# A new order for the first 259 of 1788 steps of a GLA recurrence followed by a hard-swish feed-forward

## Chip, cores and metric

The kernel runs on one core of one Trainium2 chip. The metric is device time in microseconds for one execution; the time before is the median of three runs.

## What is computed

A gated linear attention recurrence over 32 (batch, head) pairs, then a feed-forward layer with a hard-swish between two matrix products. All arrays are float32.

```python
for t in range(S):                         # B,H,S,D = 4,8,768,48
    state = alpha[:, :, t, :, None] * state + k_t (outer) v_t
    y[:, :, t] = q_t @ state
x = y.transpose(0, 2, 1, 3).reshape(3072, 384)
h = x @ w_in                               # 384 x 2048
g = h * np.clip(h + 3.0, 0.0, 6.0) / 6.0
out = g @ w_out                            # 2048 x 384
```

The kernel receives its inputs as 64-bit floats; their bit patterns are loaded and the weights are turned into float32 on the chip. That is what the `d` steps below do.

## The kernel before

The sequence is cut into 24 chunks of 128 tokens (`j`, six to a batch entry), and pairs of chunks are the 12 groups `g` of the feed-forward part. There are no loops at run time: the whole kernel is a list of 1788 words, and each word such as `tk.3.1` names a step (a small function) with its arguments. Python walks the list once and emits each step's instructions; each engine then runs its own instructions in the order of the list, and semaphores join the engines. So the list is at the same time the order on TensorE (PE), VectorE (DVE), ScalarE (ACT), GpSimd (POOL) and in SyncE's DMA queue (SP). The list stands in `run("""...""")` at L755; the table of steps is at L732.

The steps of the opening, with the line their instructions carry in the profile:

| word | engine | line | what it does |
|---|---|---|---|
| `la.j lk.j lq.j` | SP | L251, from j=6 L262 | load alpha, k, q of a chunk (192 KB) into a ring of three places; from j=6 four DMAs each |
| `lv.j.z` | SP | L272 | load v in two halves of 96 KB |
| `w.i` | SP | L162, L166 | load slice i of 16 weight slices (768 KB) into one of five landing places |
| `z.m.n` | PE | L532 | n idle matmuls of the identity, two instructions each |
| `ta tk tq .j.bank` | PE | L282 | transpose alpha, k, q into a PSUM bank |
| `ca.j` | ACT | L300 | copy transposed alpha to SBUF (from j=6 on DVE, L286) |
| `r.j`, `p.j` | DVE | L309, L320 | scans of decay and growth, both inputs in SBUF |
| `k.j`, `q.j` | DVE | L332 | scale k and q, read from PSUM in the opening |
| `kb.j`, `ck.j` | PE, ACT | L374, L378 | transpose scaled k back, copy it out |
| `sc.j`, `m.j` | PE, DVE | L346, L356 | scores, masked from PSUM |
| `qa.j.b`, `sv.j.b` | ACT | L366, L419 | place q and the state (`sv.0.0`: POOL, L415) |
| `u.j`, `sm.j.b`, `st.j` | PE, DVE, POOL | L429, L437/L439, L409 | state update |
| `ya yb`, `cy.j` | PE, ACT | L455, L464 | attention output, copied to xT |
| `d1 d2 dx .i` | ACT | L186, L196, L191 | low bits, magnitude, sign of a weight slice |
| `d3.i` | DVE | L203+L205 for slices 0, 1, 2, 4; L207+L208+L210 for the others | high bits |
| `d4.i` | POOL | L217 | integer add that ends the conversion and frees the landing place |
| `fa fb .i`, `f.g.i` | PE | L489, L478 | first product of the feed-forward, by half or whole group |
| `fr.g.i`, `fg.g.i` | ACT, DVE | L494, L498 | clip and gate |

Slices 0 to 7 are `w_in`, 8 to 15 `w_out`. Landing places are shared: `w.5` follows `w.0`, `w.8` follows `w.5`, `w.11` follows `w.8`, `w.14` follows `w.11` in place 0; `w.6`, `w.9`, `w.12`, `w.15` in place 1 and `w.7`, `w.10`, `w.13` in place 2 likewise, so such a load waits in SP's queue, with everything behind it, for the `d4` of the slice before. Four PSUM banks serve the attention steps and four the feed-forward (last number of the word). `qa.0.0` emits nothing.

The lines that walk the list:

```python
    def run(words):
        for word in words.split():
            name, *at = word.split(".")
            steps[name](*(int(x) for x in at))
```

Of the kernel before, what the change touches and what calls it, by code (L numbers as in the profile page):

```python
# [17 lines left out]
def kernel(  # L18
# [42 lines left out]
    G = 2  # L61
# [692 lines left out]
    with tc.manual_schedule():  # L754
        run("""z.0.5 z.0.3 z.0.1 z.0.8 qa.0.0 w.0 d2.0 d3.0 la.0 ta.0.0 ca.0 r.0 lk.0 tk.0.1 k.0  # L755
               z.0.2 p.0 la.1 ta.1.2 lq.0 tq.0.3 ca.1 r.1 lk.1 lv.0.0 sv.0.0 d1.0 kb.0.0 ck.0 z.0.2
               u.0.2.1 sm.0.0 sv.0.1 q.0 qa.0.1 tk.1.0 k.1 p.1 z.0.2 sc.0.2.3 m.0 la.2 ta.2.0 ca.2
               dx.0 w.2 d2.2 kb.1.0 ck.1 lq.1 r.2 sm.0.1 st.1 tq.1.2 q.1 d3.2 z.0.3 d1.2 dx.2
               lv.1.1 u.1.3.1 sv.1.0 sm.1.0 p.2 sm.1.1 sc.1.0.2 m.1 ya.0.3 yb.0 cy.0 lq.2 w.1 d1.1
               tq.2.1 q.2 d4.2 lk.2 tk.2.3 k.2 fa.2.0 d4.0 st.2 sc.2.0.2 d2.1 d3.1 m.2 dx.1 d4.1  # L760
               qa.1.1 lk.3 la.3 ta.3.1 ca.3 la.4 fa.0.1 sv.1.1 w.3 r.3 ta.4.3 ca.4 r.4 tk.3.1 k.3
               kb.2.0 qa.1.0 d2.3 ya.1.2 yb.1 cy.1 fa.1.2 lq.3 ck.2 d1.3 p.3 d3.3 lv.2.2 u.2.3.2
               sm.2.0 d4.3 fb.2 tq.3.1 q.3 fb.1 qa.2.0 sm.2.1 sv.2.0 st.3 fr.0.2.0 fg.0.2 lk.4
               tk.4.0 sv.2.1 w.5 d2.5 k.4 d3.5 d1.5 qa.3.0 d4.5 qa.2.1 sc.3.1.3 m.3 w.6 d2.6 d1.6
               d3.6 d4.6 lv.3.0 lq.4 w.7 kb.3.2 fb.0 f.0.3.3 kb.4.0 ya.2.1 ck.3 u.3.3.2 sm.3.0
# [173 lines left out]
```

## Time and profile before

| | us |
|---|---|
| median of three runs (537.22 to 537.84) | 537.36 |
| profiled execution, whole time | 537.71 |
| its span, first to last instruction | 535.6 |
| PE busy | 523.6 |
| DVE busy | 475.1 |
| ACT busy | 259.7 |
| POOL busy | 50.4 |
| granted TensorE clock, mean | 1.000 |

Busy times are sums over an engine's instructions; matmuls are pipelined and their ends are modelled, so a busy PE need not be at its peak. The opening that the change reorders ends on PE with `fa.4.3` (a group of L489 at 73.34 to 74.84 us) and on VectorE with `fg.1.6` (L498, 72.65 to 73.3 us). In the first 95 us the DMA engines move 20.0 MB, mostly 768 KB weight slices and 192 KB loads of the first chunks. Timeline rows give the start, the time taken, the engine, the line, the operation and its operands; in square brackets stands the idle time before and what ended it.

### The profile page before, as it was taken

The page shows a single profiled execution, that of the slowest core. Times are in us where ns is not written, and L with a number is a line of the kernel's source. Part 1 is how long each engine was busy: PE and PEld are TensorE (multiplying, and loading weights), DVE is VectorE, ACT ScalarE, POOL GpSimd, SP SyncE. Part 2 cuts the span into 40 slices and gives each one's busy share as a digit, 9 for nine tenths or more (in the row PEclk, how much of TensorE's full clock was granted, in tenths as well). Part 3 has the DMA queues.
Part 4 walks back from the last instruction along what each step waited for, and adds up shares of the span by engine and source line. Part 5 has one row for each costly group of instructions (what it writes and reads, how often), then busy time and mean ns, then how long its engine had stood idle before and what let it go on. Part 6 is the DMA issues. An engine that isn't in the chain of part 4 may idle for free.

```text
span 535.6 us, 15166 instructions
## 1 busy us (share of the span) xinstructions
PE 523.6 (98%) x6306; PEld 497.0 (93%) x6306; DVE 475.1 (89%) x839; ACT 259.7 (48%) x513; POOL 50.4 (9%) x71
## 2 busy tenths in 40 slices
PE   7799999999999999999999999999999999999997
PEld 7698886789999999999999999999999999999996
DVE  6999989999999899989999899999999898595381
ACT  3889864302753644543644444642634545553240
POOL 5333435000000000000010000000000000000000
PEclk9999999999999999999999999999999999999999
DMA  9998877006515155254354355055354042100001
GB/s 175 214 250 263 205 218 164 9 1 162 151 28 121 29 120 134 51 139 90 92 118 104 89 122 141 20 126 124 85 137 103 17 97 48 43 3 1 15 16 37
DMA packets 124100, 54.40 MB, mean 102 GB/s; under 512 B 83328, under 2 KB 116864, under 8 KB 124032
## 3 DMA queue, kind: packets, MB, share of 16 engines
q1 hardware_dynamic: 124032, 53.44, 42.4%
q8 instruction: 49, 0.80, 0.7%
q14 instruction: 19, 0.16, 0.1%
HBM read 44.50 MB, written 8.91 MB: 100 GB/s over the span
## 4 chain that ended last, share of the span: by engine, by line
PE 64%; DVE 20%; SPq 5%; DMA 3%; issue 3%; ACT 2%; POOL 2%; DVEq 0%; ACTq 0%; POOLq 0%
PE m_ps L703 28%; PE m_ps L600 24%; PE m_ps L478 4%; SPq L262 3%; PE t_ps L455 3%; DVE R L309 2%; DVE g_sb L498 2%; DVE A L356 2%; DMA v<-in_v_dram 1%; PE t_ps L346 1%; PE m_ps L516 1%; PE t_ps L429 1%; DVE g_sb L537 1%; DVE q L332 1%; DVE t L286 1%
## 5 line engine op out<-in xcount | busy, mean ns | idle before, releaser
L703 PE MATMUL m_ps<-w,g_sb 128*128 128x192 f32 x704 | 122.1, 327 | 0.7 <-ACT m_ps L709 0.6
L606 ACT COPY g_sb<-m_ps 128x512 f32<-128x512 f32 x110 | 63.5, 584 | 113.8 <-PE m_ps L600 97.4
L703 PEld LDWEIGHTS m_ps<-w,g_sb 128*128 128x128 f32 x704 | 113.7, 190 | 1.8 <-ACT m_ps L709 0.9
L703 PE MATMUL m_ps<-rings,g_sb 128*128 128x192 f32 x528 | 91.6, 327 | 0.6 <-ACT u L682 0.6
L703 PEld LDWEIGHTS m_ps<-rings,g_sb 128*128 128x128 f32 x528 | 85.3, 190 | 1.0 <-ACT u L682 0.9
L600 PE MATMUL m_ps<-xc,w 128*128 128x128 f32 x640 | 82.8, 277 | 0.5 <-DVE w L541 0.5
L600 PEld LDWEIGHTS m_ps<-xc,w 128*128 128x128 f32 x640 | 77.5, 192 | 1.7 <-issue 0.6
L494 ACT ACTIVATE r<-g_sb,half 128x512 f32<-128x512 f32 x80 | 56.7, 722 | 29.5 <-DVE g_sb L541 11.7
L498 DVE SCALAR_TENSOR_TENSOR g_sb<-r,g_sb 128x512 f32<-128x512 f32 x80 | 53.6, 683 | 7.2 <-ACT r L494 6.8
L600 PE MATMUL m_ps<-xT,raw 128*128 128x128 f32 x400 | 52.6, 278 | 1.0 <-ACT g_sb L606 0.9
L600 PEld LDWEIGHTS m_ps<-xT,raw 128*128 128x128 f32 x400 | 48.6, 192 | 2.0 <-ACT g_sb L606 1.4
L409 POOL TENSOR_TENSOR st<-sm,R 128x192 f32<-128x192 f32 x20 | 12.9, 644 | 354.4 <-DVE sm L439 305.6
L647 DVE TENSOR_TENSOR g_sb<-g_sb 128x512 f32<-128x512 f32 (+1 forms) x55 | 42.0, 792 | 1.4 <-PE m_ps L703 1.1
L600 PE MATMUL m_ps<-xT,w 128*128 128x128 f32 x320 | 42.0, 276 | 0.0
L600 PEld LDWEIGHTS m_ps<-xT,w 128*128 128x128 f32 x320 | 39.3, 192 | 0.1
L366 ACT COPY A<-q 48x256 f32<-48x256 f32 x88 | 35.6, 404 | 4.9 <-DVE q L332 3.7
L356 DVE TENSOR_TENSOR A<-t_ps,mask 64x256 f32<-64x256 f32 x96 | 36.0, 413 | 0.4
L478 PE MATMUL m_ps<-xT,w 128*128 128x256 f32 x144 | 32.8, 382 | 0.1
L600 PE MATMUL m_ps<-xc,raw 128*128 128x128 f32 x240 | 31.8, 276 | 0.0
L309 DVE TENSOR_TENSOR_SCAN R<-t,ones 128x516 f32<-128x516 f32 x24 | 29.6, 1235 | 1.1 <-ACT t L300 1.0
L478 PEld LDWEIGHTS m_ps<-xT,w 128*128 128x128 f32 x144 | 26.7, 190 | 3.8 <-POOL w L217 0.2
L600 PEld LDWEIGHTS m_ps<-xc,raw 128*128 128x128 f32 x240 | 29.6, 192 | 0.1
(105 smaller groups left out, 724.8 us busy)
## 6 DMA issues: line engine op xcount, KB each, us to landing
raw<-in_moe_w_out_dram SPq DMA_DIRECT2D x8, 768.0 KB, 5.2
raw<-in_moe_w_in_dram SPq DMA_DIRECT2D x6, 768.0 KB, 6.7
v<-in_v_dram SPq DMA_DIRECT2D x48, 96.0 KB, 3.0
out_dram<-oh SPq DMA_DIRECT2D x44, 96.0 KB, 1.7
far<-kq SPq DMA_DIRECT2D x64, 64.0 KB, 2.2
kb<-far SPq DMA_DIRECT2D x64, 64.0 KB, 2.0
aq<-in_alpha_dram SPq DMA_DIRECT2D x36, 96.0 KB, 2.4
qq<-in_q_dram SPq DMA_DIRECT2D x36, 96.0 KB, 2.4
```

The source lines that it names most:

```text
L262: nc.sync.dma_start(out=to[BLK * o : BLK * (o + 1), :, 0 : V * D - skip], in_=t[o // 2, :, :, skip : V * D])
L309: nc.vector.tensor_tensor_scan(out=reverse(R, n - 1, n), data0=reverse(ax, n, n), data1=reverse(ones, n, n), initial=0.0, op0=ALU.mult, op ...
L356: nc.vector.tensor_tensor(out=to[:, a], in0=sc[a][half], in1=mask[half, half].unsqueeze(1).to_broadcast([HB, NP, HB]), op=ALU.mult)
L366: nc.scalar.copy(out=to[:, a], in_=Q_t[j][64 * a : 64 * a + D, :, half])
L455: nc.tensor.matmul(y_of(j, (i + 1) // 2, p)[:, HB * b : HB * b + HB], vb[:, p, e : e + 32], A_t[j][:, b, 2 * p + a], start=(b == 0 and i = ...
L478: nc.tensor.matmul(h[:, f], w1[:, kk, o : o + C], xT_t[g][:, kk], start=(kk == 0), stop=(kk == KT - 1))
L494: nc.scalar.activation(out=to, in_=h, func=AF.Relu, bias=half, scale=1.0 / 6.0)
L498: nc.vector.scalar_tensor_tensor(out=to, in0=r, scalar=1.0, in1=h, op0=ALU.min, op1=ALU.mult)
L600: nc.tensor.matmul(acc[g][i][:, f * C : (f + 1) * C], spots[w][:, f * C : (f + 1) * C], x_of(g, x), start=(first and f == 0), stop=last, s ...
L606: nc.scalar.copy(out=slots[z], in_=acc[g][i])
L647: nc.vector.tensor_tensor(out=out, in0=in0, in1=in1, op=ALU.subtract)
L703: nc.tensor.matmul(to[g], a, rhs[:, f], start=(first and f == 0), stop=(last and f == HF - 1), skip_group_check=True)
```

## The change

The first 259 words of the list are put into another order. The words are the same, with the same arguments (so the same PSUM banks and buffers); from `sv.4.1` on the list is the same, and only its line breaks differ. Each engine thus gets the same instructions, in another order. Before, the reordered words were:

```diff
-        run("""z.0.5 z.0.3 z.0.1 z.0.8 qa.0.0 w.0 d2.0 d3.0 la.0 ta.0.0 ca.0 r.0 lk.0 tk.0.1 k.0
-               z.0.2 p.0 la.1 ta.1.2 lq.0 tq.0.3 ca.1 r.1 lk.1 lv.0.0 sv.0.0 d1.0 kb.0.0 ck.0 z.0.2
-               u.0.2.1 sm.0.0 sv.0.1 q.0 qa.0.1 tk.1.0 k.1 p.1 z.0.2 sc.0.2.3 m.0 la.2 ta.2.0 ca.2
-               dx.0 w.2 d2.2 kb.1.0 ck.1 lq.1 r.2 sm.0.1 st.1 tq.1.2 q.1 d3.2 z.0.3 d1.2 dx.2
-               lv.1.1 u.1.3.1 sv.1.0 sm.1.0 p.2 sm.1.1 sc.1.0.2 m.1 ya.0.3 yb.0 cy.0 lq.2 w.1 d1.1
-               tq.2.1 q.2 d4.2 lk.2 tk.2.3 k.2 fa.2.0 d4.0 st.2 sc.2.0.2 d2.1 d3.1 m.2 dx.1 d4.1
-               qa.1.1 lk.3 la.3 ta.3.1 ca.3 la.4 fa.0.1 sv.1.1 w.3 r.3 ta.4.3 ca.4 r.4 tk.3.1 k.3
-               kb.2.0 qa.1.0 d2.3 ya.1.2 yb.1 cy.1 fa.1.2 lq.3 ck.2 d1.3 p.3 d3.3 lv.2.2 u.2.3.2
-               sm.2.0 d4.3 fb.2 tq.3.1 q.3 fb.1 qa.2.0 sm.2.1 sv.2.0 st.3 fr.0.2.0 fg.0.2 lk.4
-               tk.4.0 sv.2.1 w.5 d2.5 k.4 d3.5 d1.5 qa.3.0 d4.5 qa.2.1 sc.3.1.3 m.3 w.6 d2.6 d1.6
-               d3.6 d4.6 lv.3.0 lq.4 w.7 kb.3.2 fb.0 f.0.3.3 kb.4.0 ya.2.1 ck.3 u.3.3.2 sm.3.0
-               fr.0.3.1 fg.0.3 fr.0.1.0 fg.0.1 qa.3.1 sv.3.0 sm.3.1 p.4 d2.7 sv.3.1 d1.7 d3.7 d4.7
-               f.0.5.0 fr.0.5.1 fr.0.0.0 fg.0.5 fg.0.0 tq.4.3 ck.4 la.5 ta.5.2 f.0.6.3 ca.5 w.4
-               d2.4 ya.3.0 yb.3 cy.3 fr.0.6.1 yb.2 cy.2 w.9 d2.9 q.4 qa.4.1 d1.4 d1.9 dx.4 la.6 w.8
-               d3.4 r.5 lk.5 w.10 d3.9 p.5 ca.6 fg.0.6 d4.9 w.12 lq.5 lv.4.1 d2.8 d3.8 f.0.7.2 d1.8
-               st.4 d4.8 d4.4 w.11 fr.0.7.0 fg.0.7 f.1.7.0 fr.1.7.1 fg.1.7 sc.4.0.2 m.4 f.1.1.1
-               fr.1.1.0 fg.1.1 f.1.3.3 fr.1.3.1 d2.10 d1.10 tk.5.3 f.1.0.2 d2.12 d3.10 d4.10 w.13
-               fg.1.3 fr.1.0.0 fg.1.0 k.5 d3.12 lq.6 f.1.6.0 f.1.2.1 u.4.1.0 sm.4.0 d1.12 d4.12
-               sv.4.0 qa.4.0 ya.4.2 fr.1.6.1 fg.1.6 w.15 tq.5.3 fa.4.3 sv.4.1 d2.11 kb.5.1 d2.13
...
+        run("""lk.0 z.0.1 z.0.8 la.0 la.1 z.0.2 ta.0.0 z.0.5 ca.0 tk.0.1 r.0 ta.1.2 w.0 k.0 lq.0
+               lv.0.0 d1.0 lk.1 w.2 ca.1 lv.1.1 la.2 lq.1 p.0 w.1 kb.0.0 ck.0 lq.2 dx.0 r.1 z.0.2
+               lk.2 tq.0.3 u.0.2.1 q.0 z.0.3 tk.1.0 qa.0.1 sm.0.0 p.1 k.1 d2.0 sc.0.2.3 sm.0.1
+               kb.1.0 la.3 m.0 st.1 z.0.3 sv.0.1 la.4 ck.1 u.1.3.1 ta.2.0 d2.2 d3.0 sm.1.0 d1.2 d3.2
+               sv.0.0 sm.1.1 ca.2 w.3 lk.3 ya.0.3 tq.1.2 d4.0 w.5 z.0.2 sv.1.0 yb.0 q.1 dx.2 qa.1.0
+               r.2 sc.1.0.2 p.2 cy.0 tq.2.1 m.1 fa.0.1 q.2 lq.3 tk.2.3 d1.1 lv.2.2 d4.2 k.2 d2.1
+               ta.3.1 lk.4 sc.2.0.2 d3.1 st.2 dx.1 ca.3 m.2 d4.1 r.3 sv.1.1 qa.1.1 fa.2.0 ta.4.3
+               d2.3 d1.3 ya.1.2 yb.1 w.6 fa.1.2 cy.1 qa.0.0 d3.3 ca.4 tk.3.1 kb.2.0 fb.1 d4.3 k.3
+               ck.2 p.3 r.4 fb.2 sv.2.0 f.0.3.3 qa.2.0 qa.2.1 u.2.3.2 d2.5 d1.5 tq.3.1 fr.0.2.0 d3.5
+               fr.0.3.1 tk.4.0 sm.2.0 d4.5 fb.0 fg.0.2 q.3 k.4 sv.2.1 f.0.5.0 sc.3.1.3 d2.6 d1.6
+               kb.4.0 d3.6 sm.2.1 qa.3.0 fr.0.1.0 qa.3.1 fg.0.3 kb.3.2 w.7 d4.6 d2.7 f.0.6.3 fg.0.1
+               st.3 fr.0.0.0 lv.3.0 m.3 sv.3.0 ck.3 u.3.3.2 d1.7 ck.4 d3.7 ya.2.1 sm.3.0 fr.0.5.1
+               d4.7 lq.4 sv.3.1 yb.2 ya.3.0 fg.0.0 yb.3 w.4 fg.0.5 f.0.7.2 cy.3 sm.3.1 fr.0.6.1 w.9
+               cy.2 d2.4 w.10 d1.4 f.1.7.0 fg.0.6 la.5 p.4 f.1.1.1 fr.0.7.0 d3.4 fg.0.7 d2.9 d2.10
+               lk.5 d3.9 d3.10 d1.9 st.4 fr.1.7.1 tq.4.3 d1.10 ta.5.2 q.4 ca.5 fr.1.1.0 lq.5 w.8
+               d4.9 f.1.0.2 fg.1.7 r.5 tk.5.3 p.5 dx.4 d4.10 w.12 la.6 fg.1.1 lv.4.1 sc.4.0.2 k.5
+               d2.8 f.1.3.3 d4.4 qa.4.0 fr.1.0.0 sv.4.0 d1.8 m.4 tq.5.3 fg.1.0 d3.8 f.1.6.0 d4.8
+               qa.4.1 fr.1.3.1 d2.12 f.1.2.1 d1.12 w.11 fg.1.3 u.4.1.0 ca.6 fr.1.6.1 w.13 ya.4.2
+               d3.12 sm.4.0 d4.12 w.15 lq.6 fa.4.3 fg.1.6 sv.4.1 d2.11 kb.5.1 d2.13 fr.1.2.0 f.1.4.2
...
```

Read by engine, the first words become: on SP `w.0 la.0 lk.0 la.1 lq.0 lk.1 lv.0 la.2 w.2 lq.1 lv.1 lq.2 w.1 lk.2` before, `lk.0 la.0 la.1 w.0 lq.0 lv.0 lk.1 w.2 lv.1 la.2 lq.1 w.1 lq.2 lk.2` after; on VectorE `d3.0 r.0 k.0 p.0 r.1 sm.0.0 q.0 k.1 p.1 m.0 r.2 sm.0.1 q.1 d3.2 sm.1.0 p.2 sm.1.1 m.1 q.2 k.2` before, `r.0 k.0 p.0 r.1 q.0 sm.0.0 p.1 k.1 sm.0.1 m.0 d3.0 sm.1.0 d3.2 sm.1.1 q.1 r.2 p.2 m.1 q.2 k.2` after; on POOL `sv.0.0 st.1 d4.2 d4.0` before, `st.1 sv.0.0 d4.0 d4.2` after.

## The prediction

> **What bounds the kernel now.** I read the page first, then windows of the opening, then VectorE, GpSimd and SyncE in order of time, then landing times.
>
> ```profile
> PE 523.6 (98%) x6306; PEld 497.0 (93%) x6306; DVE 475.1 (89%) x839; ACT 259.7 (48%) x513; POOL 50.4 (9%) x71
> ```
>
> ```profile
> 0.00:10.00 10.00, 8.53 (x50) 8.25 (x50) 5.44 (x13) 2.78 (x3) 7.13 (x20) 1.00 1.04 175
> 10.00:20.00 10.00, 6.87 (x103) 5.46 (x104) 9.75 (x18) 7.30 (x12) 0.04 (x1) 1.00 1.30 234
> 20.00:30.00 10.00, 8.64 (x207) 7.76 (x208) 9.84 (x19) 9.74 (x14) 6.84 (x5) 1.00 0.94 208
> 50.00:60.00 10.00, 9.93 (x164) 8.24 (x163) 9.80 (x15) 9.74 (x15) 4.63 (x5) 1.00 0.79 226
> 100.00:110.00 10.00, 10.00 (x156) 6.44 (x155) 10.00 (x14) 1.67 (x4) 0.00 (x0) 1.00 0.01 2
> ```
>
> The columns are window, length, busy time of PE, PEld, DVE, ACT and POOL, granted clock, DMA share, GB/s. The reader should see that the page's 98% says nothing of the opening: for the first 20 us TensorE has gaps and the DMA engines are full (share over 1), and from 10 us on VectorE has almost no idle time. The clock is 1.00 throughout. Between 22 and 85 us TensorE's own rows follow one another with under 0.3 us of idle, so both engines are full there. The opening can therefore shrink only before 22 us, in VectorE's one later idle stretch (1.16 us before the row at 72.38, waiting for `u.4`), and in instructions that are longer than their form needs:
>
> ```profile
> 20.32 0.71 DVE L203 TENSOR_SCALAR w<-w 128x768 f32<-128x768 f32 x1
> 26.08 1.09 DVE L203 TENSOR_SCALAR w<-w 128x768 f32<-128x768 f32 x1
> 29.36 1.62 DVE L309 TENSOR_TENSOR_SCAN R<-t,ones 128x516 f32<-128x516 f32 x1
> 31.11 1.22 DVE L309 TENSOR_TENSOR_SCAN R<-t,ones 128x516 f32<-128x516 f32 x1
> 75.50 0.53 DVE L207 TENSOR_SCALAR w<-w 128x768 f32<-128x768 f32 x1
> 82.32 1.75 DVE L207 TENSOR_SCALAR w<-w 128x768 f32<-128x768 f32 x1
> ```
>
> ```profile
> 22.78 3.84 POOL L217 TENSOR_TENSOR w<-w,raw 128x768 int32<-128x768 int32 x2 [2.29 <-ACT raw L191]
> 28.03 1.86 POOL L217 TENSOR_TENSOR w<-w,raw 128x768 int32<-128x768 int32 x1 [0.75 <-ACT raw L191]
> 81.65 2.01 POOL L217 TENSOR_TENSOR w<-raw 128x768 int32<-128x768 int32 x1 [0.19 <-POOL kq L257]
> ```
>
> Each long VectorE row starts while one of GpSimd's adds (`d4`, L217) runs and ends its extra time about 0.13 us before that add ends: 26.08 pays 0.38 to 0.41 (add to 26.62), 29.36 pays 0.40 (add to 29.89), 82.32 pays 1.22 (add to 83.66). VectorE steps that read PSUM (`m` L356, `q`/`k` L332, `fg` L498, `sm` L439) pass beside an add at their usual length. So a hold costs what is left of the add when a weight step (`d3`) or a scan (`r`, `p`) comes up.
>
> **The change, part by part.** Nothing is added or removed: the 259 steps that really move keep their instructions, so work is the same per engine and only idle time and holds can differ. The sum is made against the profiled execution (span 535.6, whole time 537.71) and carried as a difference to the median of 537.36.
>
> *Loads.* Landing is start plus the listed time:
>
> ```profile
> raw<-in_moe_w_in_dram SPq DMA_DIRECT2D x1, 768.0 KB, 4.9
> rings<-in_alpha_dram SPq DMA_DIRECT2D x1, 192.0 KB, 5.6
> rings<-in_k_dram SPq DMA_DIRECT2D x1, 192.0 KB, 6.3
> ```
>
> `w.0` lands at 0.74+4.9 = 5.6, `la.0` at 1.24+5.6 = 6.8, `lk.0` at 8.05; the next rows give `la.1` 9.3, `lq.0` 10.4, `lk.1` 11.5, `lv.0` 13.2, `la.2` 14.0, `w.2` 16.2. They land one behind another: about 1.2 us for each ring load, 2.2 for a weight slice, 1.7 for the two halves of `v`. The new queue in the same spacing (an estimate from these rows): `lk.0` 4.7, `la.0` 5.9, `la.1` 7.1, `w.0` 9.2, `lq.0` 10.4, `lv.0` 12.0, `lk.1` 13.2, `w.2` 15.3, `lv.1` 17.0, `la.2` 18.2, `lq.1` 19.4, `w.1` 21.5, `lq.2` 22.7, `lk.2` 23.8. So `la.0`, `la.1` and `lv.0` come earlier, and `la.2`, `lq.1`, `lk.1` and `lq.2` 1.7 to 4.2 us later.
>
> *First scan.* Idle matmuls before `ta.0.0` fall from 17 to 11: 22 of the 34 instructions that took 6.51 us, 4.2 us, done at 5.7. `ta.0.0` runs at 5.9 instead of 7.89 and `r.0`, 1.37 later by the old rows, at 7.2 instead of 9.26. But the old VectorE did `d3.0` (pitch 1.36) before that, and the new one has it later. `z.0.5` (1.9 us) now lies between `ta.0.0` and `tk.0.1`, so `k.0` starts at 8.9 and `p.0` ends at 10.6. ScalarE's `d1.0` now stands ahead of `ca.1` and waits for `w.0` (9.2): `ca.1` ends at 10.7 and `r.1` starts at 10.75, old 12.34. Counting `d3.0`, that is 10.75+1.36-12.34 = -0.23.
>
> *`k.1`.* `lk.1` (13.2) and `z.0.3` put `tk.1.0` at 13.8 and `k.1` at 14.4; VectorE is free at 14.2: +0.2.
>
> *Hold of `d3.2`.* New VectorE order: `d3.0 sm.1.0 d3.2`. The add `d4.0` needs `d3.0`, `d1.0` and `dx.0`, the last two long done, and nothing is ahead of it on GpSimd; adds start 0.13 after the VectorE row they wait for (41.34 to 41.47). It takes 1.86. `sm.1.0` covers 0.3, then `d3.2` is held to 0.13 before the add's end: 1.86-0.3 = about +1.5 (below: 0 if the add came up late, no gain possible). Behind `d3.2` stand `sm.1.1`, `q.1`, `r.2`, and `qa.1.0` and `cy.0` on ScalarE wait for them.
>
> *Hold of `r.2`.* `d4.2` needs `d3.2` (about 21.5) and ScalarE's `dx.2` (about 22.0); `r.2` comes up at 22.45: between 0 and 1.4. I take the half, +0.7, since the old `r.3` paid 0.40 where the add had 0.5 left. By the Trainium skill, page "SBUF — State Buffer", section "Who interferes with whom", whichever engine issues first keeps the shared port pair for its whole instruction and the other is blocked fully; three held rows agree to 0.13 us, but no row shows a scan coming up with a whole add ahead of it. By that rule the term would be 1.4 and the final sum below +2.2.
>
> So `k.2` ends at about 28.4, old 26.08: +2.2 by the terms (-0.23+0.2+1.5+0.7), the rest rounding. TensorE waits there for `k.2`: `sc.2.0.2` at 28.5, then in its new order `fa.2.0 ta.4.3 ya.1.2 yb.1 fa.1.2 tk.3.1 kb.2.0` by the old pitches (0.6+1.35+0.45+1.2+1.4+0.45+0.45) to 34.5, where the old one stood at 33.3 with the same steps done: **+1.2 on TensorE**. From there the old TensorE had no idle until 85 us, so nothing wins that back, and `fa.4.3` ends at 76.0, old 74.84.
>
> *VectorE behind that.* The old hold before `d3.1` goes (-0.4); `r.3` keeps its 0.4; `d3.3 k.3 p.3` puts `p.3` 0.6 after an add of 1.47 begins: +0.85; `d3.9 d3.10` back to back, with `d4.9` asking in between, 0 to 1.4, taken 0.3 since VectorE's next row follows in 0.03 us and the add only after 0.13. With the 1.16 of old idle filled: 2.2-0.4+0.85+0.3-1.16 = **+1.8**. Behind the opening VectorE is without idle from 72.4 to 123, so the later of the two frontiers is passed on, and it lies between +1.2 and +1.8: **+1.5**, 537.36+1.5 = 538.9.
>
> **The rivals.** *Faster:* the place is VectorE between `d3.0` and `k.2`; the price is those holds, 2.2 us. Without them `q.1` starts at 20.2, `k.2` ends at 26.0, TensorE runs `kb.2.0` to the end at 32.2 (old 33.3) and VectorE ends `fg.1.6` near 72.5 (old 73.25): about -1.0, 536.4. It decides as soon as the two holds sum to less than 1 us. For it: a hold is free where `sm.1.0` or `d2.2` is late anyway. Against: the rows at 26.08 and 82.32.
>
> *Late weights:* `d3.8` moves behind `fg.0.7 d3.10 fg.1.7 k.5 m.4 fg.1.1 fg.1.0` (five of 0.6 to 0.7, 2.1 and 1.5: 6.6) and ahead of `ca.6` (1.0), so `d4.8` and with it the load `w.11`, which waits for it, come 5.6 later: issue 63.57 becomes 69.2 plus the shift, landing 6.0 later at 76.7. The old `d2.11` began at 73.52. ScalarE's `d2.13 fr.1.2.0` queue behind it and `d3.11` comes 1.5 to 2 later: 540.6.
>
> *Nothing arrives:* holds are half of what I take, the early matmuls win 1 us, and the shift vanishes in the later holds (the one at 82.32 alone is 1.22): 537.4.
>
> **How the numbers follow.** Forecast 40%, faster 33%, late weights 12%, nothing arrives 15%. A measurement of this kernel tells 0.2%, 1.07 us, from no change (the three runs span 0.12%). The forecast's own range is 538.4 to 540.3; with the faster case, whose best is a full -1.6 if `la.0` lands at 5.0, and half of the late-weight case, 535.7 to 541.0 leaves out 2 in 10. Slower: 0.40+0.12 = 0.52; same 0.15; faster 0.33.
>
> **What would show it.** `r.0` (the first L309 row) near 7.2; a weight step L203 of over 1.5 us between 18 and 21; the second `r.2` scan over 1.6; TensorE idle before the third group of L346; first L489 row near 24, the last one of the opening ending near 76; `w.11`'s issue after 69. The forecast is wrong if L203 stays near 0.7, or if `la.2` and `lq.1` land as early as before.

## The result: 1.7% slower, most of it lost behind the first loads

| | before | after |
|---|---|---|
| median of five runs, us | 537.36 (537.18 to 537.84) | 547.15 (546.28 to 547.32) |
| profiled execution, whole time | 537.71 | 546.40 |
| its span | 535.6 | 544.6 |

The ratio is 1.0174, with a 95% interval of 1.0163 to 1.0186: 9.8 us were lost where 1.5 were forecast. First the page's busy times and the windows of the changed kernel, with the columns used above:

```profile
PE 526.1 (97%) x6306; PEld 498.0 (91%) x6306; DVE 480.4 (88%) x839; ACT 259.7 (48%) x513; POOL 49.9 (9%) x71
```

```profile
0.00:10.00 10.00, 7.70 (x55) 7.49 (x56) 6.35 (x15) 3.54 (x5) 6.45 (x19) 1.00 0.98 186
10.00:20.00 10.00, 7.12 (x156) 5.65 (x155) 9.82 (x16) 7.54 (x13) 2.87 (x3) 0.90 1.25 254
20.00:30.00 10.00, 7.72 (x130) 6.66 (x130) 9.41 (x16) 8.48 (x12) 3.83 (x3) 0.84 0.98 242
50.00:60.00 10.00, 9.32 (x191) 7.96 (x191) 7.81 (x13) 8.39 (x15) 1.98 (x2) 1.00 0.80 201
80.00:90.00 10.00, 9.56 (x102) 7.25 (x101) 7.61 (x13) 5.98 (x10) 3.13 (x6) 1.00 0.95 277
```

The work is the same, yet VectorE is busy 5.3 us longer (480.4 against 475.1): nearly all of it is time inside instructions that are held, as the rows below show. Between 50 and 60 us and between 80 and 90 us it is idle for over 2 us, where it had 0.2 before. TensorE's granted clock is under 1 between 10 and 30 us, which it never was in the profile of before. VectorE's rows in order of time:

```profile
6.62 1.23 DVE L309 TENSOR_TENSOR_SCAN R<-t,ones 128x516 f32<-128x516 f32 x1 [2.44 <-ACT t L300]
17.21 2.32 DVE L203 TENSOR_SCALAR w<-w 128x768 f32<-128x768 f32 x1
23.05 2.49 DVE L320 TENSOR_TENSOR_SCAN P<-t 128x516 f32<-128x516 f32 x1
28.20 0.68 DVE L203 TENSOR_SCALAR w<-w 128x768 f32<-128x768 f32 x1
56.02 0.69 DVE L498 SCALAR_TENSOR_TENSOR g_sb<-r,m_ps 128x512 f32<-128x512 f32 x1 [2.06 <-ACT r L494]
62.31 1.70 DVE L208 TENSOR_SCALAR w<-w 128x768 uint32<-128x768 uint32 x1
68.00 2.48 DVE L320 TENSOR_TENSOR_SCAN P<-t 128x516 f32<-128x516 f32 x1
89.61 1.17 DVE L286 STREAM_TRANSPOSE q<-qq 128x512 f32<-128x512 f32 x1 [2.11 <-DMA qq<-in_q_dram]
98.39 0.69 DVE L541 SCALAR_TENSOR_TENSOR raw<-w 128x512 f32<-128x512 f32 x1
```

The last of these rows in the kernel before:

```profile
89.37 0.69 DVE L541 SCALAR_TENSOR_TENSOR raw<-w 128x512 f32<-128x512 f32 x1
```

The row at 17.21 is `d3.2`, the one at 28.20 is `d3.1`, which starts when `k.2` ends (26.08 before: +2.1). The row L541 comes at 98.39 instead of 89.37: +9.0, which is the difference of the two spans. So 2.1 us were lost up to `k.2` and 6.9 between 28 and 98 us. GpSimd's adds beside the held rows:

```profile
17.15 1.84 POOL L217 TENSOR_TENSOR w<-w,raw 128x768 int32<-128x768 int32 x1 [1.94 <-DVE w L205]
22.27 2.17 POOL L217 TENSOR_TENSOR w<-w,raw 128x768 int32<-128x768 int32 x1 [3.29 <-ACT raw L191]
61.94 1.66 POOL L217 TENSOR_TENSOR w<-raw 128x768 int32<-128x768 int32 x1 [7.32 <-DVE raw L210]
67.13 2.26 POOL L217 TENSOR_TENSOR w<-w,g_sb 128x768 int32<-128x768 int32 x1
```

Against rows of the same form that no add meets, `d3.2` pays 1.64 (2.32 for 0.68), `p.2` 1.27 (2.49 for 1.22), `d3.10` 1.14 (1.70 for 0.56, in its second instruction: the row of the add `d4.9` begins at 61.94, while the first one still runs until 62.27), and `p.5` 1.26 (2.48 for 1.22).

Behind 28.2 us the account on VectorE is: idle before `k.3` 0.36, `p.3` held 0.5, idle before `d3.5` 0.72, idle before `fg.0.6` 2.06, `d3.10` held 1.14, `r.5` 0.35, `p.5` 1.26, idle before `q.6`'s transpose 2.11, `p.6` held 0.9: 9.4. From it go three costs of the old order that are not there now: `d3.1`'s hold (0.4), the idle 1.16 near 72, and the held weight step at 82.32 (1.22). That leaves 6.6 of the 6.9.

Two of these terms, the idle time before `k.3` and before `d3.5`, go with the granted clock, which is half from 28 to 31.5 us in this execution. In seven profiled executions with this order of VectorE's steps from `d3.1` to `d3.5` the clock fell between 28 and 34 us, and VectorE needs 11.73 to 11.87 us from the one step to the other; in the two where the clock was 1.00 there (`fr.0.6.1` moved, and four moves together, below) it needs 10.94 and 10.95 and has neither idle time. So the fall of the clock there costs 0.8 of the 9.8.

### The profile page after: what moved, and what is told of

It is laid out like the page before. It is cut to its first block, busy times and chain, and to the rows that moved or that the text cites. A ratio compares the mean times of both kernels' runs of the same rounds, so it can differ in the third digit from the quotient of the medians.

```text
span 544.6 us, 15151 instructions
## 1 busy us (share of the span) xinstructions
PE 526.1 (97%) x6306; PEld 498.0 (91%) x6306; DVE 480.4 (88%) x839; ACT 259.7 (48%) x513; POOL 49.9 (9%) x71
## 4 chain that ended last, share of the span: by engine, by line
PE 62%; DVE 20%; SPq 5%; DMA 5%; ACT 4%; issue 3%; POOL 1%; DVEq 0%; ACTq 0%; POOLq 0%
PE m_ps L703 27%; PE m_ps L600 24%; SPq L262 3%; PE t_ps L455 3%; DVE g_sb L498 2%; PE m_ps L489 2%; DMA qq<-in_q_dram 2%; PE m_ps L478 1%; DVE P L320 1%; DMA rings<-in_alpha_dram 1%; DVE g_sb L537 1%; PE t_ps L346 1%; PE t_ps L429 1%; DVE t L286 1%; ACT r L494 1%
## 5 line engine op out<-in xcount | busy, mean ns | idle before, releaser
L494 ACT ACTIVATE r<-g_sb,half 128x512 f32<-128x512 f32 x80 | 56.7, 722 | 29.4 <-DVE g_sb L541 11.8
L647 DVE TENSOR_TENSOR g_sb<-g_sb 128x512 f32<-128x512 f32 (+1 forms) x55 | 42.0, 793 | 1.7 <-PE m_ps L703 1.1
L320 DVE TENSOR_TENSOR_SCAN P<-t 128x516 f32<-128x516 f32 x24 | 33.2, 1385 | 0.2
```

What stands on the lines that cost most here:

```text
L320: nc.vector.tensor_tensor_scan(out=P_t[j], data0=aX[j % 2][:, 0:n], data1=ini[j % 2], initial=0.0, op0=ALU.mult, op1=ALU.add)
L494: nc.scalar.activation(out=to, in_=h, func=AF.Relu, bias=half, scale=1.0 / 6.0)
L647: nc.vector.tensor_tensor(out=out, in0=in0, in1=in1, op=ALU.subtract)
```

## Experiments

All medians are device time; each kernel was compared with before on the same chip (537.2 to 537.5). Gains are against 547.15, the changed kernel. The runs of one experiment lie 0.7 to 2.8 us apart, so a gain of about 1 us in the median is not clear by itself.

### One load ahead of three weight slices

```diff
-                qa.4.1 fr.1.3.1 d2.12 f.1.2.1 d1.12 w.11 fg.1.3 u.4.1.0 ca.6 fr.1.6.1 w.13 ya.4.2
-                d3.12 sm.4.0 d4.12 w.15 lq.6 fa.4.3 fg.1.6 sv.4.1 d2.11 kb.5.1 d2.13 fr.1.2.0 f.1.4.2
+                qa.4.1 fr.1.3.1 d2.12 f.1.2.1 d1.12 lq.6 w.11 fg.1.3 u.4.1.0 ca.6 fr.1.6.1 w.13 ya.4.2
+                d3.12 sm.4.0 d4.12 w.15 fa.4.3 fg.1.6 sv.4.1 d2.11 kb.5.1 d2.13 fr.1.2.0 f.1.4.2
```

> The changed order with one word moved: the load lq.6 goes ahead of w.11, w.13 and w.15 in SyncE's queue, as it stood before. Theory of the queue: lq.6 waits behind w.15, which waits for the add d4.12, and this is the 2.1 us in which VectorE waits for DMA qq at 89.6; then the wait goes and the time falls by about 2 us, to 545. Rival: the late weights w.11 and w.13 hold the same stretch (d3.11 and d3.13 begin right behind their magnitude steps), VectorE waits there instead, and the time stays within 0.5 us of 547.

In the order of before `lq.6` stood behind `w.11` and `w.13` and ahead of `w.15` only; this move goes further than that.

Measured: 544.71 (544.3 to 545.2), ratio 1.014 [1.0125, 1.0155], 2.4 us gained. SyncE's queue in the changed kernel, start and time taken by the issue:

```profile
77.50 3.99 SPq L166 DMA_DIRECT2D raw<-in_moe_w_out_dram  x3
81.54 3.00 SPq L262 DMA_DIRECT2D qq<-in_q_dram  x4
```

and in the experiment the load, then VectorE behind it:

```profile
67.63 2.64 SPq L262 DMA_DIRECT2D qq<-in_q_dram  x4
```

```profile
87.59 1.11 DVE L286 STREAM_TRANSPOSE q<-qq 128x512 f32<-128x512 f32 x1
88.55 1.17 DVE L320 TENSOR_TENSOR_SCAN P<-t 128x516 f32<-128x516 f32 x1
...
90.86 2.05 DVE L210 SCALAR_TENSOR_TENSOR raw<-raw,w 128x768 uint32<-128x768 uint32 x1
```

The load goes out 13.9 us earlier and the idle 2.11 is gone. The next add (`d4.11`) now holds another row, L210, by 1.1 where it held `p.6` by 0.9: that hold moves, it does not vanish. So the wait was made by the queue: `lq.6` had stood behind `w.11`, which waits for `d4.8` (done at 77.47), and `w.15`, which waits for `d4.12` (done at 81.09).

### One clip ahead of a copy on ScalarE

```diff
-                d4.7 lq.4 sv.3.1 yb.2 ya.3.0 fg.0.0 yb.3 w.4 fg.0.5 f.0.7.2 cy.3 sm.3.1 fr.0.6.1 w.9
+                d4.7 lq.4 sv.3.1 yb.2 ya.3.0 fg.0.0 yb.3 w.4 fg.0.5 f.0.7.2 fr.0.6.1 cy.3 sm.3.1 w.9
```

> The changed order with the clip fr.0.6.1 ahead of the copy cy.3 on ScalarE. Theory of the order on ScalarE: fr.0.6.1 could run at 53.6 but stands behind cy.3, which waits for yb.3 on TensorE until 54.8, and VectorE idles 2.06 us for it at 54.0 to 56.0; then fg.0.6 comes 1.6 us earlier and the time falls by 1 to 1.6 us. Rival: TensorE sets the pace there (54.6 to 71 without idle), and the time stays the same within 0.4 us.

Measured: 546.02 (545.81 to 548.01), ratio 1.0176 [1.0157, 1.0196]: no gain that the runs can tell. ScalarE in the changed kernel:

```profile
54.79 0.48 ACT L464 COPY xT<-t_ps 128x384 f32<-128x384 f32 x1 [1.51 <-PE t_ps L455]
55.29 0.69 ACT L494 ACTIVATE r<-m_ps,half 128x512 f32<-128x512 f32 x1
```

The clip `fr.0.6.1` (L494) waits behind the copy `cy.3` (L464), which waits 1.51 for TensorE. VectorE in the experiment:

```profile
54.32 0.69 DVE L498 SCALAR_TENSOR_TENSOR g_sb<-r,m_ps 128x512 f32<-128x512 f32 x1 [0.55 <-ACT r L494]
...
56.52 0.69 DVE L203 TENSOR_SCALAR w<-w 128x768 f32<-128x768 f32 x1 [0.36 <-ACT w L196]
```

`fg.0.6` starts 1.70 earlier, but two rows later VectorE waits for ScalarE again, and at the held row of `d3.10` 0.58 is left (61.73 for 62.31), of which 0.19 stood ahead of the edit already. The cause is right as to the row; the price is not the idle time, since ScalarE is the next to be late.

### Two loads moved forward among the first ones

```diff
-                lv.0.0 d1.0 lk.1 w.2 ca.1 lv.1.1 la.2 lq.1 p.0 w.1 kb.0.0 ck.0 lq.2 dx.0 r.1 z.0.2
+                lv.0.0 d1.0 lk.1 la.2 w.2 ca.1 lq.1 lv.1.1 p.0 w.1 kb.0.0 ck.0 lq.2 dx.0 r.1 z.0.2
```

> The changed order with the loads la.2 and lq.1 ahead of w.2 and lv.1 in SyncE's queue, as they stood before. Theory of the late loads: TensorE waits 1.5 us for la.2 (17.8), q.1 then comes at 20.96, and the gap lets the granted clock fall to 0.5 for 3.3 us; with the loads early, q.1 comes 1 to 2 us earlier, the first stretch at clock 0.5 goes, and the time falls by 1.5 to 3 us. Theory of the holds: d3.2 is held 1.6 us by the add d4.0 whatever loads first, so q.1 comes at most 0.5 us earlier and the time falls by less than 0.6 us.

Measured: 548.82 (548.27 to 549.56), ratio 1.0217 [1.0202, 1.0232]: 1.7 us slower than the changed kernel. Both theories missed: the time did not fall, and `d3.2` was not held whatever loads first. VectorE:

```profile
20.03 0.36 DVE L439 TENSOR_TENSOR s<-t_ps,st 128x192 f32<-128x192 f32 x1 [2.15 <-POOL w L217]
20.30 0.68 DVE L203 TENSOR_SCALAR w<-w 128x768 f32<-128x768 f32 x1
...
22.77 0.69 DVE L332 TENSOR_TENSOR q<-t_ps,P 128x512 f32<-128x512 f32 x1 [0.81 <-PE t_ps L282]
```

The idle 2.15 is put down to GpSimd, but TensorE's row shows what was late: `u.1.3.1` waited for `v`.

```profile
18.97 0.92 PE L429 MATMUL t_ps<-v,kb 64*48 64x48 f32 x32 [2.86 <-DMA v<-in_v_dram]
```

`d3.2` is not held at all (0.68), and `q.1` is nevertheless 1.8 later than in the changed kernel (20.96). The loads that went forward put `lv.1` back, for which TensorE waited 2.86 here and not at all in the changed kernel. So this run does not say what the late `la.2` costs there. The changed kernel's own rows do:

```profile
17.84 1.03 PE L282 MATMUL t_ps<-ident,rings 128*128 128x128 f32 x4 [1.54 <-DMA rings<-in_alpha_dram]
20.96 0.69 DVE L332 TENSOR_TENSOR q<-t_ps,P 128x512 f32<-128x512 f32 x1 [0.44 <-PE t_ps L282]
```

TensorE waits 1.54 for `la.2`; two steps behind, `tq.1.2` ends at 20.92, and `q.1` starts then, after 0.44 idle. The 1.64 of `d3.2` ended before that. By these rows `q.1` would come at about the same time without the hold.

### A scan behind the masking of scores (p.2)

```diff
-                r.2 sc.1.0.2 p.2 cy.0 tq.2.1 m.1 fa.0.1 q.2 lq.3 tk.2.3 d1.1 lv.2.2 d4.2 k.2 d2.1
+                r.2 sc.1.0.2 cy.0 tq.2.1 m.1 p.2 fa.0.1 q.2 lq.3 tk.2.3 d1.1 lv.2.2 d4.2 k.2 d2.1
```

> The changed order with the scan p.2 behind m.1 on VectorE, so that m.1, which reads PSUM, runs beside the add d4.2. Theory of the holds: p.2 takes 1.22 instead of 2.49, q.2 comes 1.3 us earlier, TensorE's wait of 2.04 us for it shrinks below 1 us, the second stretch at clock 0.5 goes, and the time falls by 1.2 to 2.5 us. Rival, later waits (cy.3, the weights, lq.6) set the end whatever happens here: the time stays within 0.5 us.

Measured: 544.83 (544.71 to 546.1), ratio 1.0147 [1.0132, 1.0162], 2.3 us gained. `m.1`, which reads PSUM, now runs beside the add; `p.2` and `q.2` behind it on VectorE:

```profile
24.56 1.55 DVE L320 TENSOR_TENSOR_SCAN P<-t 128x516 f32<-128x516 f32 x1
26.21 0.69 DVE L332 TENSOR_TENSOR q<-t_ps,P 128x512 f32<-128x512 f32 x1
```

`p.2` pays 0.33 instead of 1.27, and `q.2` starts 0.78 earlier (26.99 in the changed kernel). The median gained more than that row. In the trace the row L541 is 1.7 earlier (96.67 for 98.39): 0.8 stands at `d3.1`, and 1.0 comes late, where VectorE waits 1.12 instead of 2.11 before `q.6`'s transpose. That wait is the one of the load `lq.6`, not of the row that was moved.

### The same for p.5

```diff
-                d4.9 f.1.0.2 fg.1.7 r.5 tk.5.3 p.5 dx.4 d4.10 w.12 la.6 fg.1.1 lv.4.1 sc.4.0.2 k.5
-                d2.8 f.1.3.3 d4.4 qa.4.0 fr.1.0.0 sv.4.0 d1.8 m.4 tq.5.3 fg.1.0 d3.8 f.1.6.0 d4.8
+                d4.9 f.1.0.2 fg.1.7 r.5 tk.5.3 dx.4 d4.10 w.12 la.6 fg.1.1 lv.4.1 sc.4.0.2 k.5
+                d2.8 f.1.3.3 d4.4 qa.4.0 fr.1.0.0 sv.4.0 d1.8 m.4 p.5 tq.5.3 fg.1.0 d3.8 f.1.6.0 d4.8
```

> The changed order with the scan p.5 behind m.4 on VectorE, so that fg.1.1, k.5 and m.4, which read PSUM, run beside the add d4.4. Theory of the holds: p.5 takes 1.22 instead of 2.48, k.5 comes 2.5 us earlier, TensorE's wait of 1.7 us for it goes, and the time falls by about 1.3 us, to 545.8. Rival: VectorE is behind on loads and clips anyway and waits elsewhere for the time won: within 0.4 us of 547.

Measured: 545.30 (544.75 to 545.76), ratio 1.0144 [1.0129, 1.0159], 1.85 us gained.

```profile
70.44 1.23 DVE L320 TENSOR_TENSOR_SCAN P<-t 128x516 f32<-128x516 f32 x1
```

The scan has its usual length where it had 2.48, and the row L541 is 1.55 earlier (96.84): the hold of 1.25 cost at least itself.

### Idle matmuls in the two gaps, for the clock

```diff
-                kb.1.0 la.3 m.0 st.1 z.0.3 sv.0.1 la.4 ck.1 u.1.3.1 ta.2.0 d2.2 d3.0 sm.1.0 d1.2 d3.2
+                kb.1.0 la.3 m.0 st.1 z.0.3 sv.0.1 la.4 ck.1 u.1.3.1 z.0.4 ta.2.0 d2.2 d3.0 sm.1.0 d1.2 d3.2
...
-                ta.3.1 lk.4 sc.2.0.2 d3.1 st.2 dx.1 ca.3 m.2 d4.1 r.3 sv.1.1 qa.1.1 fa.2.0 ta.4.3
+                z.3.5 ta.3.1 lk.4 sc.2.0.2 d3.1 st.2 dx.1 ca.3 m.2 d4.1 r.3 sv.1.1 qa.1.1 fa.2.0 ta.4.3
```

> The changed order with idle matmuls added where TensorE waits: z.0.4 ahead of ta.2.0 and z.3.5 ahead of ta.3.1 (18 instructions, 3.4 us, in waits of 1.5 and 2.0 us). Theory of the clock: both stretches at clock 0.5 go, the L489 group at 29.4 takes 1.5 instead of 2.6, and the time falls by 1 to 1.6 us. Theory that VectorE sets the pace there: the clock is 1.00 throughout and the time stays within 0.5 us of 547, or rises by what the added matmuls overhang.

Measured: 545.12 (544.7 to 545.82), ratio 1.0143 [1.0127, 1.0158], 2.0 us gained. Windows of the changed kernel (the clock is the third value from the end):

```profile
16.00:18.00 2.00, 0.46 (x28) 0.33 (x17) 1.94 (x4) 0.83 (x2) 0.85 (x1) 0.99 1.13 278
18.00:20.00 2.00, 2.00 (x37) 1.50 (x37) 1.97 (x2) 1.05 (x3) 0.99 (x1) 0.50 1.23 274
26.00:28.00 2.00, 0.26 (x2) 0.26 (x3) 1.96 (x5) 1.09 (x1) 0.00 (x0) 1.00 1.11 282
28.00:30.00 2.00, 2.00 (x38) 1.66 (x37) 1.97 (x5) 1.49 (x4) 0.26 (x1) 0.55 1.07 351
```

and of the experiment:

```profile
18.00:20.00 2.00, 1.93 (x45) 1.60 (x44) 2.00 (x2) 1.29 (x3) 1.81 (x1) 1.00 1.19 287
...
30.00:32.00 2.00, 2.00 (x11) 2.00 (x11) 1.96 (x5) 1.95 (x4) 1.84 (x1) 0.50 1.44 176
```

The first fall of the clock is gone, the second stays. The profiled span gained only 0.6 (544.0) at a mean clock of 0.997; the three other executions had 1.000 and spans of 542.9 to 543.5. That fits a second fall that costs about 0.8, as above. But over the runs of one kernel the mean clock does not order the times: with `p.5` moved, the slowest run (545.76) had 1.000 and the fastest (544.75) 0.994. How much of the 2.0 is the clock's stays open.

### Four moves together

> The changed order with four moves together: lq.6 ahead of w.11, fr.0.6.1 ahead of cy.3, p.2 behind m.1, p.5 behind m.4. If the four causes lie one behind another on one path, their gains (2.4, 1.1, 2.3 and 1.3 if the hold of p.5 costs what it shows) add up to about 7 and the time is near 540. Rival, gains overlap because each is paid back in a later wait: 542 or more. What is then left to 537.3 belongs to the first 28 us and to the holds of d3.10 and r.5.

The edits are those of `lq.6`, `fr.0.6.1`, `p.2` and `p.5`. Measured: 541.44 (540.93 to 543.43), ratio 1.0085 [1.0065, 1.0105], 5.7 us gained, where the four alone sum to 7.6. What holds VectorE up in it:

```profile
17.45 2.32 DVE L203 TENSOR_SCALAR w<-w 128x768 f32<-128x768 f32 x1
...
34.75 2.05 DVE L320 TENSOR_TENSOR_SCAN P<-t 128x516 f32<-128x516 f32 x1
...
59.80 1.71 DVE L208 TENSOR_SCALAR w<-w 128x768 uint32<-128x768 uint32 x1
```

These are `d3.2`, `p.3` (0.83 over its 1.22) and `d3.10` (1.15 over 0.56); the row L541 stands at 92.67, 3.3 behind before, as its span does (538.9). From `d3.5` (38.05) to that row this kernel needs 54.62 us, where the changed kernel needs 58.46 (39.93 to 98.39): 3.84 less. Alone, `lq.6` took 1.96 out of this stretch, `p.5` 1.46 and `fr.0.6.1` 0.45, together 3.87. So in the traces these three lie one behind another on VectorE, and none covers another.

### The kernel before with two of its own holds taken away

```diff
-                tq.6 p.6 d2.15 d3.15 fg.1.2 d1.13 d4.13 sc.5.0.3 yb.4 f.1.5.0 fr.1.5.1 fg.1.5 tk.6
+                tq.6 p.6 d2.15 fg.1.2 d1.13 d4.13 sc.5.0.3 yb.4 f.1.5.0 fr.1.5.1 fg.1.5 d3.15 tk.6
...
-                b.0.0.1 fr.0.4.0 d3.14 k.6 q.6 ca.7 fg.0.4 d1.14 d4.14 x.0 y.1 y.10 b.0.1 y.0 y.2
+                b.0.0.1 fr.0.4.0 d3.14 ca.7 fg.0.4 k.6 q.6 d1.14 d4.14 x.0 y.1 y.10 b.0.1 y.0 y.2
```

> The order from before the change, with two of its own holds behind the opening taken out: d3.15 behind fg.1.5 (it was held 1.22 us by the add d4.13) and k.6 q.6 behind ca.7 fg.0.4 (q.6 was held 1.28 by d4.14). Theory that a hold on a full VectorE goes straight into the time: L207 at 82 takes 0.55, L332 at 93 takes 0.68, and the time falls by 1.2 to 2.5 us, to 535. Rival, TensorE sets the pace behind 85 us: within 0.4 us of 537.3.

Measured: 536.81 (536.65 to 537.65), ratio 0.999 [0.9981, 0.9999]: 0.6 us below before, and the fastest kernel of this study. VectorE is 2.1 us earlier behind the two places (its row L647 at 94.13 instead of 96.25), but TensorE is not. Its row near 127 in before and in the experiment:

```profile
127.84 1.13 PE L600 MATMUL m_ps<-xc,w 128*128 128x128 f32 x8 [0.47 <-DVE w L541]
```

```profile
127.34 1.13 PE L600 MATMUL m_ps<-xc,w 128*128 128x128 f32 x8
```

Of the 2.1 us won on VectorE only this 0.5 reaches the end: with the old order TensorE is the bound behind 85 us and waits for VectorE in this one place. The trace shows one thing more. The steps up to 72 us are those of before in the same order, yet the clock fell in this execution:

```profile
20.00:22.00 2.00, 1.68 (x66) 1.60 (x70) 1.97 (x5) 1.97 (x2) 0.21 (x1) 0.62 1.26 260
22.00:24.00 2.00, 2.00 (x66) 1.83 (x67) 1.99 (x5) 1.12 (x4) 1.57 (x1) 0.53 0.66 92
```

and at 73.6 us VectorE was 0.1 behind before. So a fall of the clock does not belong to the new order alone, and in that place it cost 0.1.

### The change cut in two at k.2

The first kernel has the new order up to `k.2` and then the old order of all words that are left; the second the old order up to `k.2` and then the new one. The place where the two orders meet in the first kernel:

```diff
...
+               r.2 sc.1.0.2 p.2 cy.0 tq.2.1 m.1 fa.0.1 q.2 lq.3 tk.2.3 d1.1 lv.2.2 d4.2 k.2 qa.0.0
+               fa.2.0 st.2 sc.2.0.2 d2.1 d3.1 m.2 dx.1 d4.1 qa.1.1 ta.3.1 ca.3 sv.1.1 r.3 ta.4.3
+               ca.4 r.4 tk.3.1 k.3 kb.2.0 d2.3 ya.1.2 yb.1 cy.1 fa.1.2 ck.2 d1.3 p.3 d3.3 u.2.3.2
...
```

> The changed order up to the step k.2 (88 words), and from there the words that are left in the order of before. It cuts the change in two at the place where the forecast ended its sum on the first loads and holds. Theory A (the loads and holds up to k.2 cost about 2 us, and most of the loss is made behind them, by waits of the later part of the new order): k.2 ends 2.1 later than before, near 28.2, as in the changed kernel, but the later waits (fr.0.6.1 behind cy.3, the held d3.10, p.5 and r.5, lq.6 behind w.15) are not there, and the old order's idle stretch of 1.16 us near 72 takes up part of the delay: fg.1.6 0.5 to 2 after the old 72.65, time 538 to 539.5. Rival B (the later part only passes on what the first part lost, its waits being taken up where the engines would have waited anyway): 545 to 547, and fg.1.6 near 79.

> The other half: the order of before up to k.2 (79 words), and from there the words that are left in the changed order. Theory A: k.2 ends as before, near 26.1, yet the later waits are all met: d3.10 and p.5 held over 1 us each, fr.0.6.1 late, q.6's load behind w.15 late; time 543 to 545.5, and fg.1.6 4 to 5.5 later than the old 72.65. Rival B: 537 to 538.5, with fg.1.6 within 1 us of 72.65. Together with the kernel that has only the new first part, the two losses should add up to about the 9.8 us of the whole change if neither covers the other.

Measured: new first part 539.21 (538.72 to 539.81), ratio 1.003 [1.0018, 1.0042], +1.9; old first part 545.74 (545.49 to 546.87), ratio 1.0158 [1.0139, 1.0177], +8.4 over 537.33. Together 10.3, the whole change 9.8: the two losses add up, and about four fifths lie behind `k.2`. VectorE with the new first part:

```profile
73.98 0.36 DVE L439 TENSOR_TENSOR s<-t_ps,st 128x192 f32<-128x192 f32 x1 [1.16 <-PE t_ps L429]
74.26 0.68 DVE L498 SCALAR_TENSOR_TENSOR g_sb<-r,m_ps 128x512 f32<-128x512 f32 x1
```

`fg.1.6` (74.26) is 1.6 later than before, and the idle time of 1.16 is still there: TensorE's `u.4` is just as late. `d3.1` starts 2.0 later (28.08) and its old hold of 0.4 is gone; the 1.6 that is left goes through unchanged to the row L541 (90.92). VectorE with the old first part meets the later waits in full:

```profile
54.80 0.69 DVE L498 SCALAR_TENSOR_TENSOR g_sb<-r,m_ps 128x512 f32<-128x512 f32 x1 [2.29 <-ACT r L494]
...
66.78 2.47 DVE L320 TENSOR_TENSOR_SCAN P<-t 128x516 f32<-128x516 f32 x1
...
88.56 1.14 DVE L286 STREAM_TRANSPOSE q<-qq 128x512 f32<-128x512 f32 x1 [2.35 <-DMA qq<-in_q_dram]
```

Where the two orders meet, near 27 us, this kernel has waits of its own (VectorE idle 0.62 and 0.98 around `d3.1`): `m.2` starts 1.3 later than before (29.13 for 27.81), which is part of its 8.4. The 7.1 that is left is near the 6.9 read off the changed kernel.

### The weight step d3.10 moved as well

To the four moves, `d3.10` was put from right behind `d3.9` to behind `q.4` and `fg.1.7`.

> The changed order with the four moves made together before (lq.6 ahead of w.11, fr.0.6.1 ahead of cy.3, p.2 behind m.1, p.5 behind m.4), and d3.10 moved from right behind d3.9 to behind q.4 and fg.1.7. Theory: the add d4.9 now runs beside q.4 and fg.1.7, which read PSUM and pass; d3.10's second instruction (L208), held 1.15 us before, has its usual 0.56, at most 0.3 of hold is left before it, and r.5 comes up before the add d4.10 and loses its hold of 0.36 too. VectorE is 0.8 to 1.5 us earlier at p.6: time near 540.3 instead of 541.4. Rival: the hold only moves to another row, or TensorE or ScalarE is late next there: 541.4 still, and L208 short but an idle row or another long row behind it.

Measured: 544.54 (542.28 to 545.1), ratio 1.0122 [1.0096, 1.0147]: 3.1 us slower than the four moves without it, so both the theory and its rival missed.

```profile
63.22 0.69 DVE L332 TENSOR_TENSOR q<-t_ps,P 128x512 f32<-128x512 f32 x1 [1.94 <-PE t_ps L282]
```

`q.4` comes first now and waits 1.94 for TensorE. The held `d3.10` had stood over that wait. Behind it `p.5` is held by 0.58 again, and VectorE waits 1.41 for ScalarE at 90.22. In the profiled execution 1.6 us were also lost ahead of the edit (`fg.0.6` at 54.20 instead of 52.56): `r.2` was held by 1.07, which it was not in the kernel with four moves, and the clock fell behind 28 us (0.9). So the price of this move is not told apart from that loss.

### The old first part with three of the moves

The second kernel of the cut, with `lq.6`, `fr.0.6.1` and `p.5` moved as above.

> The kernel with the old first part (before's order up to k.2, the changed order of the rest, 545.74) and three of the moves in that rest: lq.6 ahead of w.11, w.13 and w.15; fr.0.6.1 ahead of cy.3; p.5 behind m.4. Theory A (the later loss is made by these waits, one behind another on VectorE): the idle 2.29 before fg.0.6 falls under 0.8, p.5 has its usual 1.23 instead of 2.47, the idle 2.35 before q's transpose goes, and about 5.3 us come back (the single moves on the whole change brought 2.4, 1.1 and 1.85): 540 to 541.5. What is left above before is then the hold of L208 (1.15), of p.3 (0.83) and the seam near 27 us (about 1.2). Rival B (waits hide one another; another engine holds the rest up): under 3 us come back, 543 or more.

Measured: 542.95 (542.75 to 543.44), ratio 1.0101 [1.0084, 1.0118], 2.8 us gained on 545.74: under the rival's 3 as far as the median goes. The trace tells why. Of the three waits the one before `fg.0.6` falls to 0.55 and the two others are gone, and from `fg.0.2` (42.79) to the row L541 (94.95) VectorE needs 52.2 us instead of 56.4 (41.06 to 97.42), 4.2 less. Ahead of that, where the two orders meet, TensorE ran at half clock:

```profile
26.55 2.93 PE L489 MATMUL m_ps<-xT,w 128*128 128x128 f32 x12 [1.87 <-POOL w L217]
```

where the kernel without the moves has 26.41 and 1.60. `m.2` starts 1.7 later (30.83 for 29.13), 1.3 of it by this row. Here the clock did cost time: TensorE was what VectorE waited for next.

## Why the prediction was right in direction and wrong in size

- *Loads* and *first scan*: the spacing held. `ta.0.0` ran at 5.37 (forecast 5.9), `r.0` at 6.62 (7.2), `ta.2.0`, which waits for `la.2`, at 17.84 (18.2). `r.1` came at 9.75 instead of 10.75, so this term was a gain of 1.2 rather than 0.23. The +0.2 of `k.1` did not come either (`k.1` at 13.10 had no wait).
- *Hold of `d3.2`*: forecast 1.5, measured 1.64; but `q.1` behind it waited for TensorE and the late `la.2` in any case, so its own price is less. *Hold of `r.2`*: `d4.2` came a little too late for `r.2` and held `p.2` by 1.27 (forecast 0.7, bounds 0 to 1.4): mechanism right, next row. The Trainium skill, page "SBUF — State Buffer", section "Who interferes with whom", states that the second to issue is blocked fully; the trace agrees, with 1.78 and 1.39 us of the add ahead and holds of 1.64 and 1.27.
- The sum up to `k.2`: forecast +2.2, measured +2.1, but from other terms: -1.2 by the first scans, 1.64 and 1.27 by the two holds, and 0.44 by TensorE's lateness before `q.1`, where the forecast had -0.23, 0.2, 1.5 and 0.7. That the two sums agree to 0.1 is luck.
- What this sum is worth: the forecast gave +1.2 on TensorE, +1.8 on VectorE and 1.5 in all. The kernel with the new first part alone shows +1.6 on both (`fa.4.3` at 74.94 instead of 73.34), +1.5 in its span and +1.9 in its median. That the +1.8 fits is luck in part: it holds 0.85 and 0.3 of the later order, which this kernel does not have, and -1.16 for the idle time near 72, which was not filled. And 2 us won on VectorE do not go to the end by themselves (the kernel of before with two holds less).
- *The step that failed* is "From there the old TensorE had no idle until 85 us, so nothing wins that back", with the short sum under *VectorE behind that*. It asked what could win time back behind `k.2` and not what the new order there loses. `fa.4.3`, forecast to end at 76.0, ran from 78.57 to 80.17. The old first part with the new rest shows that loss: 8.4 us, 7.1 without the place where its two orders meet. Of the waits that make it, `d3.10` was named and mis-sized (0 to 1.4, taken 0.3, measured 1.14, and 1.15 with the four moves: the add got in between the two instructions of the step, although the second follows the first by 0.03), `p.3` was taken at 0.85 and measured 0.5 to 0.83, and `p.5` (1.26), `r.5` (0.35), `fr.0.6.1` behind `cy.3` (2.06) and `lq.6` behind `w.11` and `w.15` (2.11) were not looked for. Nor had the forecast a term for the granted clock, which it read as 1.00 throughout: 0.8 behind `k.2`. In the old order `cy.3` and `fr.0.6.1` stand in the same sequence, but `fg.0.6` came only behind `d3.9`, `p.5` and `ca.6`, at 59.08, 6.3 after the clip had ended; in the new one it is VectorE's next step. What covered the wait was moved away from it.
- *Late weights* had the right queue and a wrong victim: `w.11` went out at 77.50, not at 71, because `d3.8` meets all the waits ahead of it (73.73, 14.0 later: 6.6 and −1.0 by its place, 2.1 from the first part and 6.0 from what comes behind it, 13.7 together). First hurt was `q.6`'s transpose, whose load stood behind three slices; ScalarE's waits for slices came to 2.88 at most.
- *Faster* and *nothing arrives*: they needed holds of under 1 us and of about 1.1 us up to `k.2`; the holds were 2.9.
- The range took its upper end from one late transfer. Several waits of the later part add up on one engine, and the range had no place for that.

What stays open: the four moves leave 3.3 us in the trace, of which 1.0 stands at `k.2` already (`d3.1` at 27.10 instead of 26.08). The holds of `p.3` and `d3.10` are in the rest, but no run takes them out alone. The share of the first fall of the clock, near 18 to 22 us, was not separated either.

## What to carry to other kernels

When a list is reordered, walk the whole new stretch engine by engine and ask at each step what used to stand between it and the one it waits for; pricing only the start leaves out most of the time, as four fifths were here. A load placed behind one that waits for a buffer inherits that wait, and the list of a DMA queue has to be read for this as carefully as that of an engine. An idle or held row is worth what the next late engine leaves of it: cutting an idle time of 2.06 us to 0.55 left a gain of 0.4 at `d3.10`, and moving a held step away uncovered a wait of 1.94.

## What the runs showed of the hardware

TensorE's granted clock fell to 0.50 in the changed kernel behind 2-us windows in which TensorE was busy for 0.46 and 0.26 us. The traces show no fixed limit: it also fell behind 1.04 (`p.2` moved), and behind 1.26 and 0.98 (the kernel of before with two holds less), while it kept 1.00 behind 0.72 (`lq.6` moved) and, in the kernel before, behind 1.12 and 1.04. Each fall lasted 3.4 us; this is an estimate from the clocks of the 2-us windows (the 0.50 and 0.65 of the changed kernel's first fall are 2.0 and 1.4 us at half clock). The Trainium skill, page "TensorE: Matmul & The Clock Gate", section "Part 1: The HAM clock gate", states a clock of 4/8 after an idle window of some 3.4 us, with windows that run freely. The traces agree with the half clock, with the length, and with a fall that comes in one execution and not in another; but TensorE was not idle for 3.4 us at a stretch ahead of the two falls of the changed kernel (its waits there are 1.54 and 2.04). A fall cost from 0.1 us (the kernel of before with two holds less) over 0.8 (the changed order behind 28 us) to 1.3 in one row (2.93 for 1.60), by whether another engine waited for TensorE.
